# A gated mix of a long convolution and a spectral filter: channel transforms folded twice in f32, first stage and short convolution on 32x32 tiles, an order table for the planner

## The chip, the cores and the metric

The kernel runs on one core of one Trainium2 chip. Its five engines work side by side and meet through semaphores: TensorE (PE, with its weight loads shown as PEld), VectorE (DVE), ScalarE (ACT), GpSimd (POOL) and SyncE (SP), which issues the transfers. Each engine takes its instructions in the order in which they stand in the program. The metric is the device time of one execution in microseconds (us); lower is better.

## The reference

The input x = A_q has 2048 tokens of 640 channels. Path A is a gated long convolution along the tokens, path B a two-dimensional spectral filter of the same x, and a sigmoid of x mixes the two:

```python
g = _sigmoid((x * gate_w).sum(-1, keepdims=True))
a = _A_ref(x, A_k, A_v, A_shift_k, A_ssm_k, A_ssm_D)
b = _B_ref(x, B_w_r, B_w_i)
return g * a + (1 - g) * b
```

In path A, `k` goes through a causal convolution of four taps for each channel (`A_shift_k`), is multiplied by `v`, goes through a causal convolution of 2048 taps for each channel (an FFT of length 4096 in the reference, with `A_ssm_k`), gets `kv * A_ssm_D` added, and is multiplied by `q`. In path B, `rfft2` over tokens and channels is multiplied by `w_r + 1j * w_i` and taken back by `irfft2`. Everything is float32.

## The kernel before

The token transforms of length 2048 are split as 64 x 32, and every transform is a matmul with a constant matrix. A token is 32 n1 + n2; n2 is split in two halves of 16.

**Path B** runs once over all channels. `dfwd` (lines 469 to 498) takes two of 32 token columns at a time, 16 units in all. It transforms the 640 channels: a fold of the channels (d with d + 320) on POOL or DVE, line 470; then the folded tile is split into a high part (ACT, line 471) and a low part (line 472), and three matmuls in the type fp32r, high by high, low by high and high by low, stand for one in float32 (line 486). The logit of the gate comes out as one more column and is copied by DVE (line 491); ACT moves the rest to the array `XX` (line 498). Then come a first token stage (`b1`, matmul 526, transposing move by DVE 530), a second with the filter weights (`bs2`: matmul 546, two DVE products 553, two POOL sums 557), and the way back (`i1`: matmul 406, DVE transpose 411). `bfin_front` (matmuls 589 and 593) and `bfin` make the 16 output rows: again a split into high and low (ACT 598, DVE 599), 18 fp32r matmuls for each row (line 617), the scaling by 1 - g (ACT 621, DVE 623), the sum with path A on POOL (line 631), and the store.

**Path A** runs in five chunks of 128 channels. `kv` does the four taps in the layout channel by token: ACT takes the first tap (line 644), DVE the other three as scalar-tensor-tensor operations of 1024 elements (line 646), POOL multiplies by `v` (line 649; DVE in the first chunk), PE transposes (line 654), ACT moves (line 657). `s1` is the first token stage of the data and of the filter: four units each, each two matmuls on 64 x 128 tiles of the array (line 674) and one DVE transpose (line 677). `amid` is the second stage and the spectral product: 64 x 32 tiles (line 703), ACT copy 708, four DVE products 710, two POOL sums 717 with the result in the filter's array `YH`. `is1a` (406, 411) and `afin` (744, 747) go back to tokens. The two arrays `Y` and `YH` are the halves of `YY`, so a chunk's transforms wait for the readers of the chunk before.

The two paths meet through DRAM: path A writes to a scratch array `mad` that `bfin` loads again (line 628), or, where the path-A part comes late, `bfin` writes to `bfd` and `afin` loads that (line 750).

What sets the order: every operation is recorded with its engine, a cost and a due time (`DUE`, `OFF`), and `_Plan.order` runs them through a list scheduler with 8 PSUM banks and pools of SBUF buffers. What comes out is the order of the instructions on each engine.

One matmul of the program in float32 is two MATMUL instructions in the profile (line 703 is run 640 times by the program and stands there with x1280); one in fp32r is one.

## Time and profile before

| what | value |
|---|---|
| time, median of 3 runs (lowest, highest) | 361.31 us (360.91, 362.24) |
| profiled execution, first to last instruction | 362.2 us |
| PE busy | 300.0 us, 83% |
| DVE busy | 270.3 us, 75% |
| POOL busy | 203.6 us, 56% |
| ACT busy | 125.1 us, 35% |
| transfers | 66.89 MB, mean 185 GB/s |
| granted TensorE clock, mean | 0.959 of full speed |

The page has no other time of the profiled execution than its span, which lies between the lowest and the highest of the runs. Busy times are unions: instructions of one engine that overlap are counted once in an engine's total, but the groups by line count each for themselves, so their sum is a little above the total. A matmul's mean duration is from start to end and overlaps with its neighbours; what a group of matmuls costs is its busy time divided by the count.

### The profile page before, as it was taken

Reading aid. Unit: us, or ns where it says so; the run is one execution under the profiler, and the core shown is the slowest. Engines: PE = TensorE matmul, PEld = TensorE weight load, DVE = VectorE, ACT = ScalarE, POOL = GpSimd, SP = SyncE. Lnnn points to the kernel's source line nnn. Section 1 sums busy time; section 2 is a strip of 40 time slices with the busy share of each in tenths; the row PEclk is TensorE's granted clock in tenths of the full one; section 3 lists DMA queues with packets and bytes.
Section 4 is the critical chain, followed back from the end, with each engine's and each line's share of the span. In section 5 each row is a group of like instructions: output and inputs, shape, how many; then the busy total and the mean of one; then the engine's idle time right before and its main releaser. Section 6 shows DMA issues by size and latency. Waiting matters only on the chain.

```text
span 362.2 us, 9119 instructions
## 1 busy us (share of the span) xinstructions
PE 300.0 (83%) x3868; PEld 203.2 (56%) x3868; DVE 270.3 (75%) x304; ACT 125.1 (35%) x215; POOL 203.6 (56%) x173
## 2 busy tenths in 40 slices
...
GB/s 251 417 408 393 323 157 65 209 181 331 235 264 139 105 104 218 354 152 306 123 107 263 18 284 71 25 110 130 268 202 4 132 128 77 26 193 287 138 116 72
DMA packets 31591, 66.89 MB, mean 185 GB/s; under 512 B 2368, under 2 KB 15424, under 8 KB 30912
## 3 DMA queue, kind: packets, MB, share of 16 engines
q1 hardware_dynamic: 29840, 62.38, 51.4%
...
## 4 chain that ended last, share of the span: by engine, by line
PE 45%; DVE 22%; POOL 11%; DMA 9%; issue 6%; ACT 5%; SPq 0%; DVEq 0%; POOLq 0%; ACTq 0%
PE banks L617 11%; PE banks L703 6%; POOL YY L717 6%; PE banks L486 6%; PE banks L674 6%; DVE acc L646 5%; PE banks L406 4%; PE banks L589 4%; PE banks L744 3%; PE banks L526 3%; DVE YY L677 3%; DVE t L710 3%; DMA xl<-w 3%; DMA afin<-q 3%; ACT XX L498 2%
## 5 line engine op out<-in xcount | busy, mean ns | idle before, releaser
L717 POOL TENSOR_TENSOR YY<-t,t 128x512 f32<-128x512 f32 x40 | 55.9, 1416 | 28.6 <-DVE t L710 28.5
L486 PE MATMUL banks<-c,xr 128*128 128x324 f32 x288 | 51.4, 326 | 4.9 <-DVE YY L677 1.4
L710 DVE TENSOR_TENSOR t<-banks,hs 128x512 f32<-128x512 f32 x80 | 50.2, 679 | 6.1 <-ACT hs L708 5.4
L486 PEld LDWEIGHTS banks<-c,xr 128*128 128x128 f32 x288 | 43.7, 191 | 18.7 <-issue 10.0
L646 DVE SCALAR_TENSOR_TENSOR acc<-k,one,acc 128x1024 f32<-128x1024 f32 x27 | 47.4, 1755 | 8.9 <-ACT acc L644 8.7
L677 DVE STREAM_TRANSPOSE YY<-banks 128x1024 f32<-128x1024 f32 x40 | 47.7, 1226 | 7.4 <-PE banks L674 7.4
L703 PE MATMUL banks<-YY,s2a 64*32 64x256 f32 x1280 | 44.0, 406 | 9.2 <-DVE YY L677 2.3
L617 PE MATMUL banks<-c,xr 128*128 128x320 f32 x288 | 45.7, 318 | 2.6 <-DVE xr L599 2.6
L708 ACT ACTIVATE hs<-banks 128x512 f32<-128x512 f32 x40 | 23.9, 598 | 69.2 <-PE banks L703 52.5
L617 PEld LDWEIGHTS banks<-c,xr 128*128 128x128 f32 x288 | 43.6, 193 | 5.4 <-DVE xr L599 4.8
L498 ACT ACTIVATE XX<-banks 64x322 f32<-64x322 f32 x64 | 29.4, 460 | 31.3 <-PE banks L486 24.6
L472 POOL TENSOR_TENSOR xr<-xf,xr 128x384 fp32r<-128x384 f32 x30 | 33.5, 1130 | 10.5 <-ACT xr L471 10.3
L703 PEld LDWEIGHTS banks<-YY,s2a 64*32 64x32 f32 x1280 | 24.2, 109 | 25.6 <-DVE YY L677 3.7
L470 POOL TENSOR_TENSOR xf<-xl 128x384 f32<-128x384 f32 x30 | 34.9, 1170 | 6.2 <-DMA xl<-xT 6.0
L674 PE MATMUL banks<-hf,one 64*128 64x512 f32 x80 | 22.4, 668 | 19.2 <-POOL hf L684 13.9
L557 POOL TENSOR_TENSOR XX<-t,t 128x322 f32<-128x322 f32 x32 | 29.5, 940 | 13.1 <-DVE t L553 11.3
L684 POOL TENSOR_TENSOR hf<-hf 1x64 f32<-1x64 f32 x10 | 6.8, 680 | 41.5 <-PE banks L703 23.9
L406 PE MATMUL banks<-YY,one 32*64 32x512 f32 x320 | 23.9, 718 | 5.4 <-DVE YY L411 3.2
L553 DVE TENSOR_TENSOR t<-banks,xl 128x644 f32<-128x644 f32 x32 | 24.8, 811 | 3.5 <-POOL YY L717 2.0
L471 ACT ACTIVATE xr<-xf 128x384 fp32r<-128x384 f32 x32 | 16.4, 521 | 30.7 <-POOL xf L470 17.3
L411 DVE STREAM_TRANSPOSE YY<-banks 128x2048 f32<-128x2048 f32 x10 | 22.9, 2308 | 4.0 <-PE banks L406 4.0
L649 POOL TENSOR_TENSOR acc<-acc,v 128x1024 f32<-128x1024 f32 x8 | 19.0, 2379 | 11.2 <-PE banks L703 8.4
...
## 6 DMA issues: line engine op xcount, KB each, us to landing
...
k<-k SPq DMA_DIRECT2D x9, 704.0 KB, 5.1
...
q<-q SPq DMA_DIRECT2D x10, 512.0 KB, 5.4
v<-v SPq DMA_DIRECT2D x9, 512.0 KB, 5.9
afin<-q SPq DMA_DIRECT2D x9, 512.0 KB, 4.5
...
```

The source lines that it names most:

```text
L406: mm(p[h * 64:h * 64 + 64, j, :nd * 8], is1[r, ri, :], v[r, h * 2 + ri, :, d0:d0 + nd, :].rearrange("p m d e -> p d m e"), start=(ri == 0) ...
L470: lambda: o(sb(f, 3, 128), sb(x, 6, 128)[:, :3], sb(x, 6, 128)[:, 3:], op=OP.subtract if z else OP.add), r=[x], w=[f], new=[f, fh, fl])
L472: op(e, pool_us(384) if pool else 0.55, lambda: o(sb(fl, 384), sb(f, 384), sb(fh, 384), op=OP.subtract), r=[f, fh], w=[fl])
L486: mm(ps(p)[:, e, :NF], u[:, cj], dfc()[:, z, hl, cj, :], start=(i == 0), stop=(i == 8))
L498: act(XX[q, (b * 16 + n0) // 2, z * 161:z * 161 + 161, :].rearrange("p c e -> p e c"), src[:, :, ri * 161:ri * 161 + 161], AF.Copy)
L617: mm(eo[:, bank, :320], u[:, o:o + 128], dic()[:, hl, bank * 3 + cj, :], start=(i == 0), stop=(i == 8))
L646: op("DVE", dvs(1024), lambda j=j: stt(sb(acc, 8, 128), K(j), sh[:, c, j:j + 1], sb(acc, 8, 128), op0=OP.mult, op1=OP.add), r=[k, "one"], ...
L674: mm(ps(p)[:, b], m1[r], v[r], start=True, stop=True)
L677: op("DVE", dve(1024), lambda: nc.vector.transpose(by_col(dst, u * 32, 32), ps(p).rearrange("p b (d n) -> p d b n", n=16)), r=[p], w=YR(s, ...
L703: mm(ps(p)[j * 32:j * 32 + 32, h].rearrange("p (y r d) -> p y r d", y=2, r=2)[:, :, ri], s2a[r, k, ri * 32:ri * 32 + 32], YY[r, :, k // 2, ...
L710: op("DVE", dve(512), lambda x=x, t=t, p=p, hs=hs, e=e: tt(V(sb(t, 4, 256)[:, 2 * e:2 * e + 2]), V(ps(p)[:, :, :256]), V(sb(hs, 2, 256))[: ...
L717: op("POOL", pool_us(512), lambda ri=ri, o=o, dst=dst: ptt(dst(), T(t1, ri), T(t2, 1 - ri), op=o), r=[t1, t2], w=[("YH", m, u) for u in ra ...
```

## The change

The file is rewritten around the same transforms. What it does:

- **Channel transforms.** `fwd` takes four token columns at a time (8 units in place of 16). It folds the channels twice: 640 to 2 x 320 to 4 x 160, with four sums or differences of 640 elements (`ttop`, lines 282 and 284 of the new file). The matmuls are plain float32, on 64 x 128 pieces with 64 output partitions (line 290) and 32 x 64 tiles for the last 32 channels (line 297). The split into high and low is gone from here and from the output rows. `dic` makes two rows at a time: 8 matmuls of 160 columns and 8 on 32 x 128 tiles (lines 417, 423), ACT 430, four DVE operations 435, two sums 438. The logits of the gate are moved by ACT (line 304) and summed by four small matmuls.
- **Short convolution.** `kv` does the four taps on PE: 64 matmuls with diagonal 32 x 32 weights on all 16 tiles of 32 x 32 (line 461), accumulated in four banks. DVE multiplies by `v` out of PSUM (469); two sums of 512 elements fold the tokens (472); DVE transposes within SBUF (473). The ACT and DVE taps, the POOL product, the PE transposes and the ACT move are gone.
- **First stage.** The fold halves the transform. One unit is 16 matmuls of 512 columns on 32 x 32 tiles (line 500); there are two units each for data and filter in place of four. DVE moves the results by transposes of 2048 (504) or 1024 elements (508). `hf` folds the filter (485), and DVE adds `A_ssm_D` (482).
- **Arrays.** `YY` has three arrays that the chunks use in turn.
- **Stores.** Path A stores to the output for the first three chunks; path B adds to that by an accumulating transfer from the POOL queue (line 442), and stores the other two chunks, to which path A adds by accumulating transfers of 512 KB with runs of 512 bytes (line 576). The scratch arrays, their transfers and the POOL sums are gone.
- **Sums on two engines.** 144 fold and product sums go through `ttop`: 37 of them stand on DVE by a table (`ON_DVE`), the others on POOL.
- **Order.** `ORDER` and `SLOTS` are tables; there is no scheduler.
- `amid` (now `s2`), `is1a`, `afin`, `b1`, `bs2`, `i1` and `bfin_front` (now `bu`) keep their matmuls. `bs2` has 8 units of all 321 columns in place of 16 of half. ACT multiplies q by the gate, eight operations of 128 elements for each tile (line 559).

The core of the diff:

```diff
+ON_DVE = {(n, i, k) for n, l in {
+    "fwd": [(0, 1), (0, 4), (1, 3), (2, 1), (3, 1), (3, 2), (4, 2), (4, 3), (4, 4), (6, 2), (7, 2), (7, 3)],
...
+    "s2": [(0, 9), (2, 8), (2, 9), (3, 9), (5, 9), (6, 8), (8, 8), (8, 9), (10, 8), (12, 8), (14, 9), (18, 8), (18, 9)],
+    "dic": [(0, 9), (2, 8), (5, 8)],
...
+    def ttop(n, fn, **kw):
+
+        o = op("POOL", pool_us(n), None, **kw)
+        o.alt = dvs(n)
+        if o.key in ON_DVE:
+            o.eng, o.us = "DVE", dvs(n)
...
-    def dfwd_front(z, n):
...
-        op(e, pool_us(384) if pool else 0.55,
-           lambda: o(sb(f, 3, 128), sb(x, 6, 128)[:, :3], sb(x, 6, 128)[:, 3:], op=OP.subtract if z else OP.add), r=[x], w=[f], new=[f, fh, fl])
-        op("ACT", 0.52, lambda: act(sb(fh, 384), sb(f, 384), AF.Copy), r=[f], w=[fh])
-        op(e, pool_us(384) if pool else 0.55, lambda: o(sb(fl, 384), sb(f, 384), sb(fh, 384), op=OP.subtract), r=[f, fh], w=[fl])
...
-            h_, l_ = (sb(t, 3, 128) for t in fr[e])
-            i = 0
-            for cj in range(3):
-                for u, hl in ((h_, 0), (l_, 0), (h_, 1)):
-                    mm(ps(p)[:, e, :NF], u[:, cj], dfc()[:, z, hl, cj, :], start=(i == 0), stop=(i == 8))
...
+    def fwd(u):
+
+        unit("fwd", u)
+        x, y, p = new("L"), new("M"), [new("ps", 2), new("ps", 2)]
+        X = lambda b: sb(b, 4, 320)
+        op("SP", ISS, lambda: dma(sb(x, 1280), I["xT"][u]), w=[x], kb=655)
+        for o in (OP.add, OP.subtract):
+            ttop(640, lambda f, o=o: f(X(y)[:, (2 if o == OP.subtract else 0):][:, :2], X(x)[:, :2], X(x)[:, 2:], op=o), r=[x], w=[y])
+        for o in (OP.add, OP.subtract):
+            ttop(640, lambda f, o=o: f(X(x)[:, (2 if o == OP.subtract else 0):][:, :2], X(y)[:, 0::2], X(y)[:, 1::2], op=o), r=[y], w=[x])
+        blk = ((0, 0, 0, 162), (3, 1, 0, 162), (2, 0, 162, 161), (1, 1, 162, 161))
...
+        def pe():
+            for g_ in range(4):
+                for s, ri, o, n in blk:
+                    mm(bk(p, g_)[ri * 64:ri * 64 + 64, o:o + n], X(x)[:, s, g_ * 64:g_ * 64 + 64], df[:, 0, ri * 323 + o:ri * 323 + o + n],
...
+
+        def rest():
+            for s, ri, o, n in blk:
+                for g_ in range(4):
+                    r = slice(g_ * 32, g_ * 32 + 32)
...
+                       start=False, stop=(o > 0), tile_position=(g_ * 32, ri * 64))
...
+    def dic(v, ub):
+        unit("dic", v)
+        p, e_, t, bf = [new("ps", 2), new("ps", 2)], new("M"), new("M"), new("M")
...
+            for n in range(2):
+                U = sb(ub, 2, 640)[:, n, :512].rearrange("p (t r k) -> p t r k", t=2, r=2)
+                for b, (t_, r_) in enumerate(order):
+                    mm(bk(p, b)[:, n * 160:n * 160 + 160], U[:, t_, r_], di[:, b * 160:b * 160 + 160], start=(n == 0), stop=False)
+
+        def rest():
+            for n in range(2):
+                for b in range(4):
+                    r = slice(b * 32, b * 32 + 32)
+                    mm(bk(p, b)[:, n * 160:n * 160 + 160], sb(ub, 2, 640)[r, n, 512:], di[r, 640:800], start=False, stop=(n == 1),
+                       tile_position=(b * 32, 0))
...
+        nf = FIRST * 128
+        if nf:
+            op("POOL", 1.1, lambda: nc.gpsimd.dma_start(out[:, n0:n0 + 2, :nf], sb(bf, 2, 640)[:, :, :nf], accum_op=OP.add),
+               r=[bf] + [("oA", c, v // 4) for c in range(FIRST)], kb=1024)
+        if nf < D:
...
-    def kv(c, h, kvt):
...
-        op("ACT", 1.25, lambda: act(sb(acc, 8, 128), K(0), AF.Copy, scale=sh[:, c, 0:1]), r=[k, "one"], w=[acc], new=[acc])
-        for j in range(1, 4):
-            op("DVE", dvs(1024), lambda j=j: stt(sb(acc, 8, 128), K(j), sh[:, c, j:j + 1], sb(acc, 8, 128), op0=OP.mult, op1=OP.add),
-               r=[k, "one"], w=[acc])
...
+    def kv(c):
+        unit("kv", c)
+        k, p = new("G"), [new("ps", 2), new("ps", 2)]
+        vs = [new("V") for _ in range(2)]
+        op("SP", ISS, lambda: dma(sb(k, 2240), I["k"][c]), w=[k], kb=1147)
+        for a in range(2):
+            op("SP", ISS, lambda a=a: dma(sb(vs[a], 1024), I["v"][c, a]), w=[vs[a]], kb=524)
...
+            for tp in range(4):
+                for i in range(4):
+                    r = slice(i * 32, i * 32 + 32)
+                    for j in range(4):
+                        o = (8 * j + 3 - tp) * 64
+                        mm(bk(p, i)[j * 32:j * 32 + 32, :], dg[r, c, tp], sb(k, 2240)[r, o:o + 512], start=(tp == 0), stop=(tp == 3),
+                           tile_position=(i * 32, j * 32))
+
+        op("PE", 4 * mmu(512), pe, r=[k, "ca"], w=p, mode="32x32")
+        sds = []
+        for a in range(2):
+            v_, f_, sd = vs[a], new("T"), new("T")
+            sds.append(sd)
+            op("DVE", dve(1024), lambda a=a, v_=v_: tt(sb(v_, 2, 512), ps(p[a]), sb(v_, 2, 512), op=OP.mult), r=[p[a]], w=[v_])
+            V = lambda v_=v_: sb(v_, 16, 2, 32)
+            for s, o in enumerate((OP.add, OP.subtract)):
+                ttop(512, lambda f, s=s, o=o, V=V, f_=f_: f(sb(f_, 2, 16, 32)[:, s], V()[:, :, 0], V()[:, :, 1], op=o), r=[v_], w=[f_])
+            op("DVE", dve(1024), lambda f_=f_, sd=sd: nc.vector.transpose(sb(sd, 4, 32, 8).rearrange("p i c n -> p i n c"),
+                                                                         sb(f_, 4, 8, 32)), r=[f_], w=[sd])
+        return sds
...
+    def hf(c, a):
...
+        for s, o in enumerate((OP.add, OP.subtract)):
+            ttop(512, lambda f, s=s, o=o: f(sb(sd, 2, 512)[:, s], sb(raw, 2, 512)[:, 0], sb(raw, 2, 512)[:, 1], op=o), r=[raw], w=[sd])
+        return sd
...
-    def s1(c, s, buf, dst, u):
...
-                r = slice(b * 64, b * 64 + 64)
-                mm(ps(p)[:, b], m1[r], v[r], start=True, stop=True)
...
+    def s1(nm, c, a, sd, y):
...
+            for s in range(2):
+                for j in range(4):
+                    r = slice(j * 32, j * 32 + 32)
+                    o = ps(p[0])[:, j] if nm == "s1Y" else bk(p, j)
+                    for h in range(2):
+                        q = (h * 2 + s) * 32
+                        mm(o[q:q + 32, :], m1[r, q:q + 32], sb(sd, 2, 512)[r, s], start=True, stop=True, tile_position=(j * 32, q))
...
+        op("PE", mmu(512), pe, r=[sd, "ca"], w=p, mode="32x32")
...
+        cs = slice(c * 128, c * 128 + 128)
+        if c < FIRST:
+            op("SP", ISS, lambda: dma(out[:, n0:n0 + 8, cs], Q()), r=[qt], w=[("oA", c, n0 // 8)], kb=524)
...
+            op("POOL", 1.1, lambda: nc.gpsimd.dma_start(out[:, n0:n0 + 8, cs], Q(), accum_op=OP.add),
+               r=[qt] + [("oB", v) for v in range(n0 // 2, n0 // 2 + 4)], kb=800)
...
+    slots = iter(SLOTS)
+    for b in plan.bufs:
+        b.slot = next(slots)
     with tc.manual_schedule():
-        for o in ops:
-            o.fn()
+        for i in ORDER:
+            plan.ops[i].fn()
```

What the tables make of the order is seen at three places. On DVE at the start, before, the names are the taps of the first chunk (`acc`, `q`), the input tile `k` and the gate columns `gs`:

```order
L646 SCALAR_TENSOR_TENSOR acc_63<-k_61,one,acc_63 128x1024
L423 TENSOR_SCALAR gs<-one 128x3
L424 SCALAR_TENSOR_TENSOR gs<-one,gs 128x2
L425 SCALAR_TENSOR_TENSOR gs<-one,gs 128x2
L426 TENSOR_SCALAR gs<-one,two 128x1
L427 TENSOR_TENSOR gs<-gs 128x1
L646 SCALAR_TENSOR_TENSOR q_84<-c_86,one,q_84 128x1024
L646 SCALAR_TENSOR_TENSOR acc_63<-k_61,one,acc_63 128x1024
```

In the changed kernel `V` holds v and the product, `L` and `M` the folds of x, `cc` and `gt` the gate columns, `T` the folded tokens:

```order
L469 TENSOR_TENSOR V_69<-banks,V_69 128x1024
L282 TENSOR_TENSOR M_64<-L_62 128x640
L267 TENSOR_SCALAR cc<-cc 128x8
L268 TENSOR_TENSOR gt<-cc 128x2x2
L269 TENSOR_TENSOR gt<-cc 128x2x2
L270 TENSOR_TENSOR cc<-gt 128x2x2
L271 TENSOR_TENSOR cc<-gt 128x2x2
L284 TENSOR_TENSOR L_62<-M_64 128x640
L469 TENSOR_TENSOR V_70<-banks,V_70 128x1024
L284 TENSOR_TENSOR L_62<-M_64 128x640
L473 STREAM_TRANSPOSE T_74<-T_72 128x4x8x32
```

The first DVE instruction was a tap that needs a loaded tile and ACT's first tap; now it is the product out of PSUM, which needs PE's 64 matmuls of the short convolution.

On DVE in the second stage of the first chunk, before; `t` are the products, `xf` and `xr` the folded channels and their low part, `lg` the logits:

```order
L710 TENSOR_TENSOR t_80<-banks,hs_77 128x512
L710 TENSOR_TENSOR t_79<-banks,hs_78 128x512
L710 TENSOR_TENSOR t_80<-banks,hs_78 128x512
L710 TENSOR_TENSOR t_81<-banks,hs_77 128x512
L470 TENSOR_TENSOR xf_71<-xl_76 128x384
L710 TENSOR_TENSOR t_82<-banks,hs_77 128x512
L710 TENSOR_TENSOR t_81<-banks,hs_78 128x512
L472 TENSOR_TENSOR xr_70<-xf_71,xr_69 128x384
L491 COPY lg<-banks 128x2
L710 TENSOR_TENSOR t_82<-banks,hs_78 128x512
```

And now, where line 541 is the sum of products that stood on POOL, 282 a channel fold, 482 and 485 work on the filter:

```order
L534 TENSOR_TENSOR M_66<-banks,H_77 128x512
L534 TENSOR_TENSOR M_67<-banks,H_77 128x512
L482 TENSOR_TENSOR V_70<-V_70 128x16
L282 TENSOR_TENSOR M_65<-L_63 128x640
L534 TENSOR_TENSOR M_67<-banks,H_76 128x512
L485 TENSOR_TENSOR T_73<-V_70 128x512
L534 TENSOR_TENSOR M_68<-banks,H_77 128x512
L482 TENSOR_TENSOR V_71<-V_71 128x16
L534 TENSOR_TENSOR M_64<-banks,H_77 128x512
L534 TENSOR_TENSOR M_66<-banks,H_76 128x512
L541 TENSOR_TENSOR YY<-M_66,M_67 128x2x2x128
```

The copies of the logits are gone from between the products; sums and folds that read two SBUF tiles have come there.

On POOL at the end, before, `v` and `acc` hold path B's rows and `xl` path A's:

```order
L631 TENSOR_TENSOR acc_63<-acc_63,xl_76 128x512
L631 TENSOR_TENSOR v_62<-v_62,xl_75 128x512
L751 TENSOR_TENSOR q_83<-q_83,hf_65 128x1024
L631 TENSOR_TENSOR v_62<-v_62,xl_73 128x640
L631 TENSOR_TENSOR acc_63<-acc_63,xl_75 128x640
L631 TENSOR_TENSOR v_62<-v_62,xl_73 128x640
L631 TENSOR_TENSOR acc_63<-acc_63,xl_76 128x640
L631 TENSOR_TENSOR v_62<-v_62,xl_74 128x640
```

And now, where 442 and 576 are the accumulating transfers, 438 the sums of path B's rows and 541 the sums of products of the last chunk:

```order
L442 DMA out_dram<-M_66 128x2x384
L541 TENSOR_TENSOR YY<-M_64,M_68 128x2x2x128
L438 TENSOR_TENSOR M_64<-M_67 128x2x320 x2
L442 DMA out_dram<-M_64 128x2x384
L541 TENSOR_TENSOR YY<-M_68,M_66 128x2x2x128 x2
L541 TENSOR_TENSOR YY<-M_65,M_67 128x2x2x128 x2
L576 DMA out_dram<-V_70 128x8x128
L576 DMA out_dram<-V_69 128x8x128
L541 TENSOR_TENSOR YY<-M_66,M_68 128x2x2x128 x2
L576 DMA out_dram<-V_71 128x8x128
L576 DMA out_dram<-V_70 128x8x128
```

The last four accumulating transfers stand in POOL's queue around the last sums of products; before, POOL's end held path-B sums alone, and the stores went out from SP.

882 lines of the change are left out of this document (305 added, 577 removed), and 39 rows, old and new, of tables (ORDER, SLOTS).

## The prediction

> **What bounds the kernel now.** I read the busy time by stage first, then the waits, then the groups by line. The table by stage has a row for each stretch, and in it the busy us of each engine with its instructions; the last row has the totals.
>
> ```profile
> core 0: us, PE busy (x) PEld busy (x) DVE busy (x) ACT busy (x) POOL busy (x), PEclk, DMA share, GB/s
> 0.00:8.00 8.00, 0.00 (x0) 0.00 (x0) 0.00 (x0) 2.40 (x3) 0.20 (x4) 1.00 0.75 252
> 8.00:270.00 262.00, 215.94 (x2828) 130.02 (x2836) 220.94 (x234) 90.18 (x162) 171.30 (x146) 0.95 0.62 207
> 270.00:358.00 88.00, 84.08 (x1050) 73.20 (x1032) 48.57 (x71) 32.54 (x52) 32.14 (x23) 0.98 0.36 117
> 358.00:362.30 4.30, 0.00 (x0) 0.00 (x0) 0.80 (x1) 0.00 (x0) 0.00 (x0) 0.70 0.20 76
> sum 362.30, PE 300.02 PEld 203.22 DVE 270.32 ACT 125.12 POOL 203.65; mean PE 75.01 PEld 50.81 DVE 67.58 ACT 31.28 POOL 50.91
> ```
>
> Nothing runs on PE and DVE in the first 8 us. From 8 to 270 us PE (215.9 of 262) and DVE (220.9) are almost equally full, with POOL at 171.3, a share of 0.65. From 270 to 358 us PE alone is the bound: 84.1 of 88, a share of 0.955, and DVE is half idle. So in three quarters of the span a gain on one engine alone is worth little, and in the last quarter only PE counts. The longest wait of DVE in the table of waits is this:
>
> ```profile
> DVE lg L491 <- ACT XX L498: 13.7, 8, 2.2
> ```
>
> DVE's copy of the gate's logit stands in its queue behind ACT's move of the same banks, and DVE is idle 13.7 us for it. Without that wait DVE's share from 8 to 270 us is 220.9 / (262 - 13.7) = 0.89.
>
> One more thing bounds DVE. In the timeline from 100 to 112 us, start and duration in the first two columns, a tap on DVE that reads two SBUF tiles lasts 5.78 us while POOL runs one operation after the other:
>
> ```profile
> 103.81 5.78 DVE L646 SCALAR_TENSOR_TENSOR acc<-k,one,acc 128x1024 f32<-128x1024 f32 x1
> ...
> 105.30 1.27 POOL L717 TENSOR_TENSOR YY<-t,t 128x512 f32<-128x512 f32 x1
> ...
> 106.53 1.97 POOL L470 TENSOR_TENSOR xf<-xl 128x384 f32<-128x384 f32 x2
> ...
> 108.47 1.32 POOL L684 TENSOR_TENSOR hf<-hf 1x64 f32<-1x64 f32 x1
> ```
>
> DVE's products that read PSUM do not stretch: the view of line 710 has their shortest, median and longest within 46 ns.
>
> ```profile
> L710 DVE TENSOR_TENSOR t<-banks,hs x80: 647/680/693, 34.6 to 299.2; 128x512 f32<-128x512 f32 x80
> ```
>
> **The change part by part.** PE, from the groups by line (busy us, then mean ns of one):
>
> ```profile
> L486 PE MATMUL banks<-c,xr 128*128 128x324 f32 x288 | 51.4, 326 | 4.9 <-DVE YY L677 1.4 <-issue 1.2 <-DVE YY L411 0.9
> ...
> L617 PE MATMUL banks<-c,xr 128*128 128x320 f32 x288 | 45.7, 318 | 2.6 <-DVE xr L599 2.6
> L703 PE MATMUL banks<-YY,s2a 64*32 64x256 f32 x1280 | 44.0, 406 | 9.2 <-DVE YY L677 2.3 <-ACT XX L498 2.0 <-DVE lg L491 1.9
> ...
> L406 PE MATMUL banks<-YY,one 32*64 32x512 f32 x320 | 23.9, 718 | 5.4 <-DVE YY L411 3.2 <-DVE lg L491 2.2
> ...
> L674 PE MATMUL banks<-hf,one 64*128 64x512 f32 x80 | 22.4, 668 | 19.2 <-POOL hf L684 13.9 <-DVE lg L491 3.0 <-DVE YY L677 2.3
> L674 PE MATMUL banks<-kvt,one 64*128 64x512 f32 x80 | 21.5, 662 | 1.9 <-ACT XX L498 1.3 <-DVE YY L677 0.3 <-ACT kvt L657 0.2
> L744 PE MATMUL banks<-YY,is2a 128*64 128x128 f32 x320 | 19.7, 277 | 0.9 <-DVE YY L411 0.9
> ...
> L589 PE MATMUL banks<-c,XX 128*128 128x128 f32 x128 | 18.8, 290 | 0.0
> ...
> L654 PE MATMUL banks<-one,acc 128*128 128x128 f32 x72 | 10.0, 284 | 3.8 <-POOL acc L649 2.3 <-DVE t L553 1.1 <-DVE YY L677 0.4
> ```
>
> The fp32r transforms (51.4 and 45.7), the first stage (22.4 and 21.5) and the transposes (10.0) go: 151.0 of 300.0, leaving 149.0. What comes is float32, two passes for each matmul.
> - Folded forward transform, 8 units: 16 matmuls of 162 columns that run in pairs. Line 744 runs pairs of 128 columns at 19.7 / 160 = 0.123 us a pass, so 162 cost 0.156, and 8 pairs in 2 passes 2.49 us. The rest is 2 sets of 8 tiles of 32 x 64; line 406 runs such a set of 512 columns in 23.9 / 40 = 0.597 us, so 162 cost 0.189, four times 0.76. Together 3.25 x 8 = 26.0.
> - Output rows, 8 units: 16 passes of 160 columns at line 589's 18.8 / 128 = 0.147 us for 128, so 2.94; the rest on four row tiles 4 x 0.187 = 0.75. 3.69 x 8 = 29.5.
> - Short convolution and first stage: packs of 16 tiles of 32 x 32, which no row shows. The nearest have 8 tiles: 0.597 a pass in line 406, and 44.0 / 160 = 0.275 for 256 columns in line 703, so 0.55 for 512. I take 0.575, as the tiles have run side by side in both. Below it stands 21.5 / 40 = 0.54, a stream of 512 columns in line 674; above it 1.19, if 8 tiles run and then the other 8. The convolution has 8 passes (4.6 us), five times: 23.0. The first stage has 20 units of 2 passes: 23.0.
>
> PE's sum is 149.0 + 101.5 = 250.5 us; with the bounds 248 to 300.
>
> The Trainium skill, in "TensorE: Matmul & The Clock Gate", section "Measured speedup vs the span model", gives 16 tiles of 32 x 32 a speedup of 10.6, not 16, so a pack lasts 1.51 single matmuls. With line 589's rate (0.588 for 512 columns) that is an estimate of 0.89 a pass and a PE sum of 275.5; no run here shows it yet.
>
> DVE and what bears on it:
>
> ```profile
> L677 DVE STREAM_TRANSPOSE YY<-banks 128x1024 f32<-128x1024 f32 x40 | 47.7, 1226 | 7.4 <-PE banks L674 7.4
> L646 DVE SCALAR_TENSOR_TENSOR acc<-k,one,acc 128x1024 f32<-128x1024 f32 x27 | 47.4, 1755 | 8.9 <-ACT acc L644 8.7
> ...
> L599 DVE TENSOR_TENSOR xr<-banks,xr 128x640 fp32r<-128x640 f32 x16 | 13.1, 822 | 10.6 <-ACT xr L598 10.5
> ...
> L747 DVE TENSOR_TENSOR q<-banks,q 128x1024 f32<-128x1024 f32 x10 | 12.2, 1215 | 1.9 <-PE banks L744 1.9
> ...
> L646 DVE SCALAR_TENSOR_TENSOR q<-c,one,q 128x1024 f32<-128x1024 f32 x3 | 3.8, 1278 | 0.0
> ...
> L491 DVE COPY lg<-banks 128x2 f32<-128x2 f32 x16 | 2.4, 149 | 14.9 <-ACT XX L498 13.7 <-PE banks L674 0.9 <-PE banks L486 0.3
> L445 DVE TENSOR_TENSOR c<-gs,c 128x2 fp32r<-128x2 f32 x4 | 2.4, 631 | 0.0
> L470 DVE TENSOR_TENSOR xf<-xl 128x384 f32<-128x384 f32 x2 | 2.0, 1016 | 0.0
> L649 DVE TENSOR_TENSOR q<-q,q 128x1024 f32<-128x1024 f32 x1 | 2.0, 2014 | 0.0
> ...
> L631 DVE TENSOR_TENSOR acc<-acc,xl 128x640 f32<-128x640 f32 x1 | 0.8, 826 | 0.0
> ```
>
> The taps (47.4, 3.8), the low parts (13.1), the logits (2.4) and the early small groups (2.4, 2.0, 2.0) go: 73.1 of 270.3, leaving 197.2. Still smaller groups that also go are left in, so this errs high. Added are ten products out of PSUM (1.215 each, line 747: 12.2), ten transposes in SBUF (none in the trace; 47.7 / 40 = 1.19 by line 677: 11.9), and 37 sums that read two SBUF tiles: 16 of 640 at 0.825 (line 631 on DVE, POOL idle then), 21 of 512 in proportion at 0.66, and ten tiny ones at 0.15, together 28.6. That is 249.9 us before the loss to POOL. A tap into `acc` has a mean of 1755 ns, and the three into `q`, in the first chunk when POOL has hardly begun, 1278: some 0.48 us each are lost while POOL works. The transposes, products and `bs2` that stay keep their price.
>
> POOL, which these 47 operations meet:
>
> ```profile
> L717 POOL TENSOR_TENSOR YY<-t,t 128x512 f32<-128x512 f32 x40 | 55.9, 1416 | 28.6 <-DVE t L710 28.5 <-PE banks L674 0.2
> ...
> L631 POOL TENSOR_TENSOR v<-v,xl 128x640 f32<-128x640 f32 x3 | 4.7, 1563 | 11.2 <-DVE v L623 10.3 <-ACT xl L629 1.0
> ...
> L453 POOL DMA_DIRECT2D c<-dfc x2 | 1.9, 938 | 0.0
> ```
>
> It has 27 sums at 1.416, 33 of 640 at 1.56, 15 of 642 at the same, 32 of 512 at 1.25 and 12 transfers to issue at 0.94: 38 + 52 + 23 + 40 + 11 = 164 us, a share of 0.51 in some 323 us. The loss of 0.48 us was at 0.65; at 0.51 it is 0.375, and 47 times that is 17.6. DVE's sum is 267.5; with the bounds of no loss and of one whole POOL operation (1.56) each, 250 to 323.
>
> The Trainium skill, in "SBUF — State Buffer", section "SBUF: two separate sides", says that DVE and GpSimd share a pair of ports under an exclusive lock, which a DVE operation takes if it has two SBUF inputs. The 5.78 us row agrees; by the rule the ten transposes in SBUF are spared, and if they were not, they would add an estimated 10 x 0.375 = 3.8 us.
>
> The start and the end:
>
> ```profile
> 1.65 0.42 SPq L641 DMA_DIRECT2D c<-k  x1
> ...
> 13.88 3.79 PE L674 MATMUL banks<-hf,one 64*128 64x512 f32 x8 [13.88 <-POOL hf L684]
> ```
>
> ```profile
> c<-dfc POOLq DMA_DIRECT2D x2, 966.0 KB, 18.3
> ...
> c<-k SPq DMA_DIRECT2D x1, 704.0 KB, 6.2
> ...
> out_dram<-q SPq DMA_DIRECT2D x1, 512.0 KB, 3.8
> ```
>
> ```profile
> 358.83 0.33 SPq L632 DMA_DIRECT2D out_dram<-acc  x1
> ```
>
> The third transfer of 704 KB, behind some 0.9 MB, lands at 1.65 + 6.2 = 7.85 us, 1.6 MB in all. The constants and k of the changed kernel are 448 and 1120 KB by their tiles, so PE can begin at 7.7. Its 4.6 us become 6.2, as the first eight matmuls of line 674 took 3.79 us in place of 8 x 0.27. DVE's first instruction waits for that: 13.9 us, in place of some 8. POOL's folds and the loads run meanwhile, but nothing on DVE does.
>
> At the end the last store was issued at 358.83, and the span is 362.2: 3.4 us. Now POOL issues it (0.94) and it adds to what is there. Such a landing is not in the trace: a plain store of the same 512 KB took 3.8, a POOL transfer in the crowded start 18.3. I take two plain landings, 7.6, as it moves the old values too; the end is 8.5 us (4.7 to 19).
>
> At no cost I count the accumulating transfers that wait in POOL's queue for path A's stores: what stands behind them are folds of the next chunk, and POOL is half idle; uncovered, the first costs a landing, 3.8 us. The scratch transfers that go were hidden, with the DMA engines at 0.62. ACT (125 us) loses more than it gets.
>
> **The sum.** The engines are now evenly loaded to the end, so the stage from 270 us goes, and the stage before is the pattern. With the logit's wait gone, the next to be late for DVE are ACT's copies of the products, which remain. DVE: 267.5 / 0.89 + 13.9 + 8.5 = 323 us. PE, as a check: 250.5 / (215.9 / 262 = 0.824) + 7.7 + 8.5 + 1.2 for the last product = 321. I forecast 323. The page gives no time of the profiled execution but its span, 362.2, which is 0.9 above the median of 361.31; that is below what I can resolve.
>
> **The rivals.**
> - *Better packed.* The table order fills DVE as the last stage filled PE, 0.955: 267.5 / 0.955 + 22.4 = 303 us. For it speaks that POOL has slack now; against it that PE and DVE are both nearly full, and that convolution, transforms and first stage take four of eight banks where most took two.
> - *Tiles by halves, the case on the other side.* The 16 tiles run 8 at a time, on PE in lines 461 and 500. 80 passes x 0.615 = 49 us: PE 299.5 / 0.824 + 17.4 = 381 us, slower. It decides from a PE sum of (362.2 - 17.4) x 0.824 = 284, which is 0.99 us a pass. For it: nothing here runs more than 8. Against it: 8 tiles cost no more than one stream. By the skill's 0.89 the time would be an estimated 352, between the two.
> - *DVE starves behind POOL.* Every one of the 47 waits out a whole POOL operation: 323 / 0.89 + 22.4 = 385 us. It decides from 1.1 us each. Against it: a loss of 0.48 at a busier POOL.
> - *No gain*: the old share of 0.843 stays and several ends add up, about 361.
>
> **How the numbers follow.** The forecast has 0.64 (from 303, no loss to POOL, to 340, DVE's share at 220.9 / 262 = 0.843), better packed 0.20, tiles 0.08, starving 0.06, no gain 0.02. The range of 298 to 350 holds the forecast and most of the better case; the three others and the far tail of the better one stay outside. A measurement can tell about 0.5%, 1.8 us, from no change. Faster takes the first two and the milder end of the tiles: 0.86; same 0.03; slower 0.11.
>
> **What would show it.** Right: DVE busy about 268 and PE about 250 us; the convolution at 4.6 us for 128 matmuls and the first stage at 1.15 for 32; the DVE sums of 512 at about 1.0 us; DVE's first operation near 14 us; 8 to 9 us from the last product to the end. Wrong: packs above 1 us a pass; DVE sums that stretch over whole runs of POOL; a share of DVE below 0.8 or above 0.95 after the start.

## The result and the profile after

The changed kernel takes 348.52 us (median of three runs, 345.36 to 350.55) against 361.31 before. The ratio is 0.962, with a 95% interval of 0.953 to 0.972; one of the three runs was disturbed and is not in it. The forecast was 323: the direction was right, and the gain is 13 us in place of 38. The profiled execution is the one of 345.36 us, with a span of 343.6.

The page of the changed kernel begins with the span and the busy time of each engine:

```profile
span 343.6 us, 10756 instructions
...
PE 266.1 (77%) x4850; PEld 155.4 (45%) x4850; DVE 263.0 (77%) x282; ACT 81.4 (24%) x188; POOL 170.5 (50%) x123
```

The sums of work are near those of the forecast: PE 266.1 (250.5 forecast, bounds 248 to 300), DVE 263.0 (267.5), POOL 170.5 (164). The table by stage is cut where DVE's first and last operations stand:

```profile
core 0: us, PE busy (x) PEld busy (x) DVE busy (x) ACT busy (x) POOL busy (x), PEclk, DMA share, GB/s
0.00:12.90 12.90, 5.84 (x128) 2.52 (x128) 0.00 (x0) 0.00 (x0) 1.76 (x5) 1.00 0.87 340
12.90:270.00 257.10, 211.68 (x3746) 124.58 (x3754) 211.51 (x220) 61.25 (x141) 129.04 (x89) 0.94 0.48 155
270.00:334.30 64.30, 48.58 (x992) 28.28 (x974) 51.45 (x64) 20.20 (x47) 38.16 (x28) 0.97 0.39 75
334.30:343.60 9.30, 0.00 (x0) 0.00 (x0) 0.02 (x1) 0.00 (x0) 1.56 (x2) 0.69 0.96 113
```

DVE begins at 12.9 us (13.9 forecast) and the end is 9.3 us (8.5 forecast). Between them DVE works 211.5 + 51.5 of 321.4 us, a share of 0.818 where the forecast had 0.89. PE's share from its first matmul at 7.1 to its last at 333.0 is 266.1 / 325.9 = 0.816. Two engines are equally full, and each is idle nearly a fifth of the time. If their intervals are laid over one another, neither runs for 18.8 us, nearly all of it at the start and the end, so both run together for 266.1 + 263.0 - (343.6 - 18.8) = 204.3 us, PE alone for 62 and DVE alone for 59. Between start and end there is hardly a moment in which both are idle, but for 121 us only one of them works: they take turns.

DVE's waits in the changed kernel (us in total, times, longest):

```profile
DVE V L469 <- PE banks L461: 17.7, 5, 12.9
DVE M L534 <- ACT H L532: 9.7, 12, 2.4
DVE XX L339 <- PE banks L335: 9.5, 7, 6.3
DVE YY L508 <- PE banks L500: 8.8, 5, 3.0
DVE V L571 <- PE banks L568: 7.3, 5, 2.3
```

The wait for ACT at the logit, 13.7 us before, is gone. In its place stand many waits for PE, at nearly every step that reads PSUM. The groups that the forecast priced without a row (busy us, mean ns, idle before):

```profile
L500 PE MATMUL banks<-T,ca 32*32 32x512 f32 x640 | 30.9, 641 | 11.0 <-DVE XX L259 3.2 <-ACT lg L304 2.0 <-DVE M L534 1.9
...
L461 PE MATMUL banks<-G,ca 32*32 32x512 f32 x640 | 25.1, 633 | 8.7 <-DMA G<-k 7.1 <-DVE M L361 1.0 <-DVE YY L508 0.7
...
L473 DVE STREAM_TRANSPOSE T<-T 128x1024 f32<-128x1024 f32 x10 | 20.4, 2072 | 0.1
...
L541 DVE TENSOR_TENSOR YY<-M,M 128x512 f32<-128x512 f32 x13 | 11.9, 924 | 0.1
...
L442 POOL DMA_DIRECT2D out_dram<-M x8 | 10.2, 1277 | 1.5 <-POOL M L438 1.5
...
L576 POOL DMA_DIRECT2D out_dram<-V x4 | 6.2, 1597 | 12.9 <-DVE V L571 12.9
```

The first stage costs 30.9 / 20 = 1.55 us a unit in place of 1.15, and the convolution 5.0 in place of 4.6. For the first stage the timeline of the changed kernel tells why; the first two columns are the start and the duration:

```profile
59.96 0.15 PEld L500 LDWEIGHTS banks<-T,ca 32*32 32x32 f32 x8 [0.23 <-issue]
59.96 2.14 PE L500 MATMUL banks<-T,ca 32*32 32x512 f32 x32
...
60.98 0.21 PEld L500 LDWEIGHTS banks<-T,ca 32*32 32x32 f32 x24 [0.87 <-ACT XX L305]
...
295.49 1.16 PE L500 MATMUL banks<-T,ca 32*32 32x512 f32 x32
```

At 295.5 us the pack of 16 tiles runs as one and takes 1.16 us, the forecast's price. At 60.0 only a part of it starts, and the rest waits until ACT has emptied its bank. The stream is then paid twice, 2.14. Banks are not the only reason: at 75.0 us the second half waits for a sum of POOL. Twelve of the twenty units take 1.14 to 1.25 us, two some 1.9 (at a granted clock of 0.57 from 184 to 188 us), and six, which start in parts or while a convolution still runs, 1.8 to 3.1 of busy time. The five convolutions take 5.84, 4.64, 5.42, 4.46 and 4.79 us; matmuls of the first one last up to 1058 ns, those of the other four 587 to 612.

The clock has a part in PE's sum. By its records in the trace PE worked some 29 of its 266 us at half clock (26 of 300 before), and there a matmul of line 500 lasts 945 to 1056 ns in place of 584 to 612.

The last chunk of the changed kernel is a chain with nothing beside it:

```profile
319.41 1.86 DVE L541 TENSOR_TENSOR YY<-M,M 128x512 f32<-128x512 f32 x2
...
320.82 5.39 PE L254 MATMUL banks<-YY,ca 32*64 32x512 f32 x64 [4.57 <-DVE YY L541]
...
324.58 4.51 DVE L259 STREAM_TRANSPOSE YY<-banks 128x2048 f32<-128x2048 f32 x2 [3.30 <-PE banks L254]
...
329.15 3.85 PE L568 MATMUL banks<-YY,is2a 128*64 128x128 f32 x64 [2.94 <-DVE YY L259]
331.23 1.23 DVE L571 TENSOR_TENSOR V<-banks,V 128x1024 f32<-128x1024 f32 x1 [2.14 <-PE banks L568]
...
334.62 1.55 POOL L576 DMA_DIRECT2D out_dram<-V  x1 [0.31 <-DVE V L571]
```

### The profile page after: what moved, and what is told of

Its sections match the earlier page's. It is cut to its first block, busy times and chain, and to the rows that moved or that the text cites. A ratio compares the mean times of both kernels' runs of the same rounds, so it can differ in the third digit from the quotient of the medians.

```text
span 343.6 us, 10756 instructions
## 1 busy us (share of the span) xinstructions
PE 266.1 (77%) x4850; PEld 155.4 (45%) x4850; DVE 263.0 (77%) x282; ACT 81.4 (24%) x188; POOL 170.5 (50%) x123
## 5 line engine op out<-in xcount | busy, mean ns | idle before, releaser
L534 DVE TENSOR_TENSOR M<-banks,H 128x512 f32<-128x512 f32 x80 | 50.6, 683 | 10.0 <-ACT H L532 9.7
L541 POOL TENSOR_TENSOR YY<-M,M 128x512 f32<-128x512 f32 x27 | 38.9, 1460 | 23.3 <-DVE M L534 20.8
L527 PE MATMUL banks<-YY,s2a 64*32 64x256 f32 x1280 | 44.3, 402 | 5.2 <-DVE YY L508 2.5
L532 ACT ACTIVATE H<-banks 128x512 f32<-128x512 f32 x40 | 23.9, 598 | 71.5 <-PE banks L527 55.3
L438 POOL TENSOR_TENSOR M<-M 128x640 f32<-128x640 f32 x13 | 20.7, 1590 | 38.8 <-DVE M L435 27.3
L559 ACT ACTIVATE V<-V,g 128x128 f32<-128x128 f32 x80 | 24.2, 388 | 66.1 <-DMA V<-q 66.1
L500 PE MATMUL banks<-T,ca 32*32 32x512 f32 x640 | 30.9, 641 | 11.0 <-DVE XX L259 3.2
L485 POOL TENSOR_TENSOR T<-V 128x512 f32<-128x512 f32 x18 | 25.0, 1398 | 24.2 <-DVE V L482 22.4
L254 PE MATMUL banks<-YY,ca 32*64 32x512 f32 x320 | 25.8, 690 | 9.3 <-DVE YY L541 4.6
L461 PE MATMUL banks<-G,ca 32*32 32x512 f32 x640 | 25.1, 633 | 8.7 <-DMA G<-k 7.1
L508 DVE STREAM_TRANSPOSE YY<-banks 128x1024 f32<-128x1024 f32 x20 | 24.3, 1231 | 8.8 <-PE banks L500 8.8
L472 POOL TENSOR_TENSOR T<-V 128x512 f32<-128x512 f32 x14 | 21.5, 1543 | 13.4 <-DVE V L469 13.4
L361 DVE TENSOR_TENSOR M<-banks,L 128x642 f32<-128x642 f32 x32 | 24.1, 813 | 1.0 <-DMA L<-w 0.5
L504 DVE STREAM_TRANSPOSE YY<-banks 128x2048 f32<-128x2048 f32 x10 | 23.0, 2305 | 1.6 <-PE banks L500 1.5
```

What stands on the lines that cost most here:

```text
L254: mm(p[h * 64:h * 64 + 64, j, :nd * 8], is1[r, ri, :], v[r, h * 2 + ri, :, d0:d0 + nd, :].rearrange("p m d e -> p d m e"), start=(ri == 0) ...
L461: mm(bk(p, i)[j * 32:j * 32 + 32, :], dg[r, c, tp], sb(k, 2240)[r, o:o + 512], start=(tp == 0), stop=(tp == 3), tile_position=(i * 32, j * ...
L485: ttop(512, lambda f, s=s, o=o: f(sb(sd, 2, 512)[:, s], sb(raw, 2, 512)[:, 0], sb(raw, 2, 512)[:, 1], op=o), r=[raw], w=[sd])
L500: mm(o[q:q + 32, :], m1[r, q:q + 32], sb(sd, 2, 512)[r, s], start=True, stop=True, tile_position=(j * 32, q))
L504: op("DVE", dve(2048), lambda: nc.vector.transpose(by_col(YY[:, :, y], a * 64, 64), ps(p[0]).rearrange("p j (d n) -> p d j n", n=8)), r=p, ...
L508: op("DVE", dve(1024), lambda b=b: nc.vector.transpose(by_col(YY[:, :, y], a * 64 + b * 32, 32), ps(p[b]).rearrange("p q (d n) -> p (q d) ...
```

## The experiments

All ratios are to the kernel before, on the same chip; the changed kernel stands at 0.962 (0.953 to 0.972). The differences show only the parts that change, with long lines shortened.

**What bounds it: less work on one engine.** The first run takes work from PE.

```diff
-            for tp in range(4):
+            for tp in range(2):
...
-            for s, ri, o, n in blk:
+            for s, ri, o, n in ():
...
-            for n in range(2):
+            for n in ():
```

> The changed kernel with less work on PE and the same instructions elsewhere: the convolution has two taps of four, and the second part of the forward transform (line 297) and of the output rows (line 423) is left out. By the groups of the changed kernel that is 25.1 / 2 = 12.5, 8.2 and 6.4 us, 27 of PE's 266. The changed kernel takes 345 to 349 us. DVE bounds it, as forecast, and PE has slack: no more than 2 us less, 343 to 348. PE bounds it: 27 / 0.83 = 32 less, about 314. They run in turn, as the eight banks let neither run far ahead (in the trace PE runs alone 62 us, DVE alone 59, both together 204): each us counts between 0.23 (62 / 266) and a half, 6 to 14 less, 332 to 341.

Measured: 338.22 us, 0.933 (0.927 to 0.938).

```profile
PE 248.6 (74%) x4146; PEld 140.5 (42%) x4146; DVE 261.6 (78%) x282; ACT 82.0 (24%) x188; POOL 169.9 (51%) x123
```

PE's busy time fell by 17.5 us (not by the 27 that the groups had promised), and the span by 8.1, to 335.5: 0.46 for each. The second run takes work from DVE (the memsets at the start only give the tiles a value, 3.6 us in time in which DVE would wait).

```diff
-nc.vector.transpose(sb(sd, 4, 32, 8).rearrange("p i c n -> p i n c"), sb(f_, 4, 8, 32))
+nc.vector.transpose(sb(sd, 1024)[:, :32], sb(f_, 1024)[:, :32])
...
+        for t in plan.T:
+            tc.nc.vector.memset(t, 0.0)
```

> The changed kernel with less work on DVE and the same instructions elsewhere: the ten transposes in SBUF (line 473, 2.07 us each) move 32 elements of 1024, so the first stage of path A reads old data. That is some 19 of DVE's 263 us. DVE bounds it: 19 / 0.82 = 23 less, 322 to 326. PE bounds it: nothing, 344 to 349. In turn: each us counts between 0.22 (59 / 263) and a half, 4 to 10 less, 336 to 344.

Measured: 343.18 us, 0.949 (0.945 to 0.954), a span of 340.2.

```profile
PE 263.2 (77%) x4850; PEld 154.7 (45%) x4850; DVE 249.9 (73%) x286; ACT 81.4 (24%) x188; POOL 171.1 (50%) x123
```

Without the memsets DVE lost 16.7 us and the span 3.4: 0.2 for each. By the medians the two figures are 0.59 and 0.32; the runs of the changed kernel lie 5 us apart, so they are rough, and which engine's us weighs more is not firm. Neither engine bounds the kernel alone; both "in turn" numbers came. The forecast's formula, DVE's sum over a fixed share, would have given 20 us here.

**The sums' engine.**

```diff
-ON_DVE = {(n, i, k) for n, l in {
...
-}.items() for i, k in l}
+ON_DVE = set()
```

> The changed kernel with all 144 folding sums on POOL, in the same order: DVE loses 37 sums, 37.9 of 263 us, and POOL gets 37 times some 1.45, 54 more, 224 in all. DVE bounds it: 37.9 / 0.82 = 46 less, about 300. In turn, with POOL in nobody's way: 8 to 19 less, 328 to 340. The sums' own length counts, as each sum that was put on DVE is one that the next stage waits for (0.9 there, 1.45 on POOL, and behind what POOL has in its queue): 0 to 15 more, 346 to 362.

Measured: 357.45 us, 0.986 (0.981 to 0.990), 9 slower than the changed kernel.

```profile
PE 272.4 (77%) x4850; PEld 158.8 (45%) x4850; DVE 236.4 (66%) x245; ACT 81.7 (23%) x188; POOL 210.9 (59%) x160
```

DVE has 26.6 us less to do and the kernel is slower. Its table of waits says where the time goes (line 277 is 284 of the changed kernel):

```profile
PEld banks L283 <- POOL L L277: 14.4, 7, 7.8
...
PE banks L283 <- POOL L L277: 10.7, 5, 6.9
...
DVE T L466 <- POOL T L465: 8.2, 5, 2.3
```

In the changed kernel PE's matmuls wait 3 us for POOL in all, and DVE not at all. Here, what counts is when a sum is ready for the step behind it, not whose busy time it is in.

**The accumulating transfers.**

```diff
-op("POOL", 1.1, lambda: nc.gpsimd.dma_start(out[:, n0:n0 + 8, cs], Q(), accum_op=OP.add),
+op("SP", ISS, lambda: dma(out[:, n0:n0 + 8, cs], Q()),
...
-op("POOL", 1.1, lambda: nc.gpsimd.dma_start(out[:, n0:n0 + 2, :nf], sb(bf, 2, 640)[:, :, :nf], accum_op=OP.add),
+op("SP", ISS, lambda: dma(out[:, n0:n0 + 2, :nf], sb(bf, 2, 640)[:, :, :nf]),
```

> The changed kernel with the twelve accumulating transfers of POOL made plain stores that SP issues, so the output holds one path's part only and not the sum. POOL loses 16.4 us of issues, and the last store lands as a plain one. The end alone counts: 1.56 to issue and 6.9 to land become 0.4 and 4.1, 4 less, 341 to 345. The queue counts too (DVE waits 4.5 us for an M buffer that such a transfer reads, and folds stand behind the transfers on POOL): 8 to 14 less, 331 to 339. Nothing less: the last landing is not what ends the span, 344 to 349.

Measured: 342.07 us, 0.944 (0.940 to 0.949). The span after DVE's last operation is 4.1 us in place of 9.3, so 5.2 of the 6 us between the medians are the end itself, as the first theory had it. The two profiled spans are only 2.2 apart (341.4 and 343.6): what lies ahead of the end is 3 us longer here. So nothing shows that the transfers' wait in POOL's queue costs time, as forecast.

**The step that gave 0.89, tried alone in the kernel before.**

```diff
-op("DVE", 0.16, lambda: nc.vector.tensor_copy(lg[:, z, n0:n0 + 2], ps(p)[:, :, 322]),
+op("DVE", 0.16, lambda: act(lg[:, z, n0:n0 + 2], ps(p)[:, :, 322], AF.Copy),
```

> The kernel before, with the copy of the gate's logit (line 491) on ACT in place of DVE; the order of everything else stays. This tries the step of the forecast that took DVE's wait of 13.7 us as time that is free once the copy leaves DVE. If it is free, DVE's share from 8 to 270 us becomes 0.89 and the kernel before takes 361.3 - 13.7 = 348. If the wait is only where DVE stands while PE and ACT are behind, it moves to the next instruction of DVE, and the time is 357 to 362.

The "DVE" in the call is a label of the planner; in the profile the sixteen copies run on ACT.

Measured: 361.14 us, 0.997 (0.994 to 1.000). Its longest waits of DVE, and its stage from 8 to 270 us:

```profile
DVE v L623 <- PE banks L617: 11.9, 6, 3.5
DVE YY L677 <- PE banks L674: 10.9, 7, 5.2
DVE xr L599 <- ACT xr L598: 10.5, 13, 1.0
...
DVE t L710 <- ACT hs L708: 7.1, 9, 2.4
```

```profile
8.00:270.00 262.00, 219.84 (x2908) 131.54 (x2908) 223.88 (x220) 92.36 (x179) 170.83 (x146) 0.96 0.61 207
```

The wait of 13.7 us is gone from the table, and the time stays. DVE's share in this stage went from 0.843 to 223.9 / 262 = 0.855, not to 0.89. The idle time moved to the next instructions that need PE: the transposes of line 677 wait 10.9 us where they waited 7.4.

**The order.** The whole table is worked out anew, by moving single steps, buffers and sums between places and keeping what made a timetable of the measured lengths shorter. The steps are the same. Not all stand on the same engine, though: 29 of the folding sums are on DVE in place of 37, and only nine of these are the same ones. Steps 226 to 232 are the filter's load, its folds and its first stage.

```diff
-ORDER = [
-    2, 203, 205, 51, 0, 204, 226, 206, 7, 6, 52, 211, 212, 53, 287,
...
+ORDER = [226, 227, 228, 229, 51, 2, 230, 231, 232, 52, 53, 54, 55, 203,
...
-SLOTS = [
-    1, 1, 0, 6, 0, 1, 0, 6, 0, 2, 4, 6, 0, 3, 0, 2, 0, 0, 0, 2, 1, 3,
...
+SLOTS = [0, 3, 4, 6, 1, 0, 6, 2, 1, 3, 0, 2, 1, 2, 4, 2, 1, 4, 4, 6, 0, 0,
```

> The changed kernel with the same instructions in another order, with other buffers and with 29 of the folding sums on DVE in place of 37: the table was worked out anew by the lengths that the trace of the changed kernel shows. The lengths written in the code make PE's sum 205 us where the trace shows 266 (the convolution 3.4 in place of 5.0, the first stage 0.85 in place of 1.5, a transpose in SBUF 1.22 in place of 2.07). If the table's wrong lengths are why PE and DVE run in turn, the time falls by 20 to 29, to 320 to 329, with PE and DVE together for over 215 us in place of 204. If the eight banks and the chain of the steps make them run in turn whatever the order, 340 to 349.

Measured: 323.04 us, 0.891 (0.887 to 0.895). This kernel's lines are 48 lower, as its tables are shorter (437 is 485 of the changed kernel). Its page, its stage between DVE's first and last operations, and its start:

```profile
PE 259.0 (80%) x4850; PEld 151.8 (47%) x4850; DVE 257.6 (80%) x274; ACT 81.3 (25%) x188; POOL 180.1 (56%) x131
```

```profile
4.70:313.80 309.10, 259.04 (x4850) 151.81 (x4850) 257.46 (x274) 80.04 (x187) 178.32 (x126) 0.96 0.52 156
```

```profile
4.77 1.29 DVE L437 TENSOR_TENSOR T<-V 128x512 f32<-128x512 f32 x2
...
7.34 2.02 PE L452 MATMUL banks<-T,ca 32*32 32x512 f32 x32 [7.34 <-DMA ca<-ca]
...
9.46 2.38 DVE L460 STREAM_TRANSPOSE YY<-banks 128x1024 f32<-128x1024 f32 x2 [3.41 <-PE banks L452]
...
11.90 5.82 PE L413 MATMUL banks<-G,ca 32*32 32x512 f32 x128 [2.53 <-DVE YY L460]
...
17.76 1.23 DVE L421 TENSOR_TENSOR V<-banks,V 128x1024 f32<-128x1024 f32 x1 [1.60 <-PE banks L413]
```

The first transfer is now a filter of 520 KB; in the changed kernel the constants (448 KB) and k (1120 KB) come first. DVE folds the filter at 4.8 us, the first stage runs at 7.3 when the constants have landed, and the convolution follows at 11.9, behind DVE's move of the first stage's result. Both engines together: 259.0 + 257.6 - (321.9 - 17.3) = 212 us. The overlap grew by 8 and not by the 11 that I named, but the sums on PE and DVE shrank by 7 and 5 us too. On DVE there are fewer sums. On PE it is not the packs (lines 461 and 500 had 56.1 us, and have 57.7 here) but lines 254 and 527, which fell from 38.8 and 44.3 us to 33.1 and 41.6. The granted clock does not explain the gain: 0.947 here, 0.942 in the changed kernel. What the sums' new engines are worth without the new order was not tried; all of them on POOL was slower, as above.

**The control: the same search with the lengths of the code.**

```diff
-    2, 203, 205, 51, 0, 204, 226, 206, 7, 6, 52, 211, 212, 53, 287,
...
+    51, 52, 226, 7, 227, 228, 229, 2, 230, 203, 53, 206, 54, 8, 9, 10,
```

> The control to the run with the table worked out anew: the same search, as long and from the same start, but with the lengths that stand in the code (205 us for PE) in place of those of the trace; the instructions are the same, 31 of the folding sums stand on DVE. If the wrong lengths made the table of the changed kernel slow, this one is slow too, 340 to 349. If the table was only searched too little, or for queues and transfers that behave otherwise than the chip's, most of the gain comes here as well, 323 to 332, and the right lengths are worth only what is left.

Measured: 326.80 us, 0.902 (0.895 to 0.909).

```profile
4.70:312.50 307.80, 254.93 (x4850) 146.08 (x4850) 265.94 (x276) 81.18 (x188) 177.92 (x124) 0.98 0.52 156
```

My reason for the new table was wrong: the lengths in the code are not what held the table back. With them the search finds nearly all of the gain (the intervals of the two ratios just touch, 0.887 to 0.895 and 0.895 to 0.909). This table has 31 sums on DVE, and its profiled execution had more clock, 0.970. The table of the changed kernel, with its choice of engines for the sums, is simply a poor one for its work.

**Start and rest.** The first 70 steps of the changed kernel's table are kept, and the rest is worked out anew.

```diff
-    291, 17, 223, 32, 224, 301, 33, 292, 225, 293, 302, 247,
...
+    291, 17, 223, 32, 33, 292, 34, 224, 225, 63, 64, 35,
```

> The changed kernel's instructions with the first 70 steps of its table kept as they are (so DVE still waits for the first convolution, some 13 us) and the rest of the table worked out anew by the lengths of the trace, as in the run that took 323.0. In that run DVE's first operation came at 4.8 us in place of 12.9, and from DVE's first operation to its last it was 309 us in place of 321. If both parts add up, this run keeps the 12 and gives back the 8: 330 to 333. If the start alone made the difference, 340 to 348. If DVE's late start is made up for later, 322 to 327.

Measured: 333.08 us; the ratio is 0.927 with a wide interval (0.899 to 0.955), as runs on this chip scattered more.

```profile
14.90:323.00 308.10, 259.23 (x4722) 152.89 (x4722) 267.41 (x279) 79.53 (x187) 170.14 (x120) 0.93 0.48 142
```

By the median both parts add up, as 330 to 333 was the expectation for that; the interval alone would allow the other two theories as well. In the profiled executions from DVE's first operation to its last it is 308.1 us in place of 321.4, and the late start remains (14.9). This table has 34 sums on DVE. Here DVE's share is 267.4 / 308.1 = 0.868.

**The transposes in SBUF.** The sources of the changed kernel by shortest, median and longest (ns):

```profile
L473 DVE STREAM_TRANSPOSE T<-T x10: 1976/2064/2215, 20.1 to 267.4; 128x1024 f32<-128x1024 f32 x10
```

```profile
L541 DVE TENSOR_TENSOR YY<-M,M x13: 645/694/1772, 60.9 to 320.6; 128x512 f32<-128x512 f32 x13
```

The sums of two SBUF tiles stretch to 2.7 times their shortest; the transposes hardly at all. They cost 2.06 us always, so this is not POOL. One run writes half of them densely.

```diff
-sb(sd, 4, 32, 8).rearrange("p i c n -> p i n c")
+sb(sd, 4, 32, 8).rearrange("p i c n -> p i n c") if a else sb(sd, 4, 8, 32)
```

> The changed kernel with half of the transposes in SBUF (line 473, the first of each chunk's two) writing their 1024 columns one after another in place of every eighth column, so the first stage of path A reads its columns in another order. If the stride makes them cost 2.06 us in place of 1.22 (line 508, out of PSUM), the five dense ones take about 1.2 and the five others 2.06. If it is the source in SBUF, all ten stay at 2.0 to 2.1. The time falls by 0 to 2, 343 to 349.

Measured, one run: 349.15 us. In its timeline a strided one and a dense one stand three us apart:

```profile
20.34 2.05 DVE L473 STREAM_TRANSPOSE T<-T 128x1024 f32<-128x1024 f32 x1
...
23.02 1.25 DVE L473 STREAM_TRANSPOSE T<-T 128x1024 f32<-128x1024 f32 x1
```

The five dense ones take 1.20 to 1.25 and the others 2.04 to 2.14. It is the stride of the write (eight elements, 32 bytes), neither the source nor the lock. The next run uses that, and lets PE read with the stride.

```diff
-sb(sd, 2, 512)[r, s]
+sb(sd, 4, 8, 32)[r, 2 * s:2 * s + 2].rearrange("p i n c -> p i c n")
```

> The changed kernel, its order kept, with all ten transposes in SBUF (line 473) writing one column after another, and the first stage of path A (line 500) reading every 32nd column in its place, so that the result stays the reference's. DVE loses 10 x 0.85 = 8.5 us. In turn, at 0.22 to 0.5 for each us: 2 to 4 less, 341 to 346. DVE bounds it: 10 less, 335 to 339. If PE reads with a stride at a lower rate, the ten units of line 500 grow (1.15 undisturbed) and the gain is lost, 346 to 352.

Measured: 351.40 us, 0.974 (0.967 to 0.980): nothing gained.

```profile
L500 PE MATMUL banks<-T,ca 32*32 32x512 f32 x640 | 39.5, 836 | 10.4 <-DVE XX L259 2.9 <-DVE M L534 2.1 <-ACT lg L304 2.0
...
L473 DVE STREAM_TRANSPOSE T<-T 128x1024 f32<-128x1024 f32 x10 | 12.1, 1220 | 0.8 <-POOL T L472 0.8
```

DVE saves 8.3 us and PE pays 8.6: undisturbed units of path A take 2.1 us in place of 1.15. That fits two engines in turn, where a us on PE weighs about as much as one on DVE.

**Both together, and a variant.** The edit of the run before, and a table that starts with the filter again:

```diff
-    2, 203, 205, 51, 0, 204, 226, 206, 7, 6, 52, 211, 212, 53, 287,
...
+    226, 227, 228, 51, 52, 53, 54, 229, 2, 230, 231, 232, 203, 206,
```

> Both together: the dense transposes with the strided first stage, and a table worked out by the lengths of the trace with 1.24 for these transposes. The run with the new table alone took 323.0. If DVE's 8.5 us count as they did by turns (0.28 a us), 320 to 321; if the better packed order lets DVE bound, 8.5 / 0.87 less, 313 to 315; if the stride costs PE what it gives DVE, 322 to 326.

Measured: 314.36 us, 0.869 (0.864 to 0.874), the fastest of all and within the second range.

```profile
PE 263.6 (84%) x4850; PEld 149.6 (48%) x4850; DVE 253.1 (81%) x276; ACT 81.0 (26%) x188; POOL 176.7 (56%) x129
```

It is not shown that DVE bounds here, as that range supposed: besides the edit the table is another one, and the granted clock was 0.974 in place of 0.947 in the run of 323.0. What each is worth was not taken apart.

The variant gives the strided read to the transpose out of PSUM.

```diff
-nc.vector.transpose(by_col(YY[:, :, y], a * 64, 64), ps(p[0]).rearrange("p j (d n) -> p d j n", n=8))
+[nc.vector.transpose(by_col(YY[:, :, y], a * 64 + i * 32, 32),
+    ps(p[0])[:, :, i * 256:i * 256 + 256].rearrange("p j (n c) -> p c j n", c=32)) for i in range(2)]
```

> The ten transposes in SBUF write one column after another, as in the run of 314.4 us, but it is now the transpose out of PSUM after the first stage of path A (line 504) that reads every 32nd column, in two halves, in place of PE (a pack then cost 2.1 in place of 1.15); the table is worked out by the trace's lengths. PE gets back some 8 us of the 36 in line 500, DVE pays 0.15 for each of ten splits. If DVE reads PSUM with a stride at its usual rate: 308 to 313. If such a read costs double, as the strided write in SBUF did, DVE grows by 20 and the time is 318 to 326.

Measured: 319.74 us, 0.892 (0.880 to 0.905). That lies in the second range, but not for its reason:

```profile
L500 PE MATMUL banks<-T,ca 32*32 32x512 f32 x640 | 27.0, 622 | 15.1 <-DMA ca<-ca 10.2 <-DVE XX L259 1.9 <-DVE YY L259 1.2
...
L504 DVE STREAM_TRANSPOSE YY<-banks 128x1024 f32<-128x1024 f32 x20 | 23.6, 1223 | 1.7 <-PE banks L500 1.7
```

The read out of PSUM with the stride costs nothing (1223 ns for 1024, where 2048 without it took 2305), and PE got its time back (36.3 to 27.0 in line 500). Yet the profiled span, 313.9, is no shorter than the 313.1 of the run before, and the median is longer. PE begins 2.8 us later, and another table differs in much else; why it is not faster stays open.

## Why the prediction was wrong

The sum was DVE / share + start + end. Term by term, forecast and measured:

| term | forecast | measured |
|---|---|---|
| DVE's sum | 267.5 | 263.0 |
| of it ten transposes in SBUF | 11.9 | 20.4 (line 473) |
| of it folding sums with the loss to POOL, tiny ones included | 46.2 | 40.3 |
| of it what was kept, and the ten products | 209.4 | 202.3 |
| PE's sum | 250.5 | 266.1 |
| of it forward, rows, convolution, first stage | 26.0, 29.5, 23.0, 23.0 | 29.2, 27.2, 25.1, 30.9 |
| DVE's first operation | 13.9 | 12.9 |
| the end | 8.5 | 9.3 |
| **DVE's share between** | **0.89** | **0.818** |

With 263.0 / 0.89 + 12.9 + 9.3 the time would be 317.7; with 0.818 it is 343.6. The errors of the other terms bring the sum from 323 to 317.7, so by the formula the whole miss of 26 us between 317.7 and the profiled span is in the share. With the 0.855 that the kernel before had without the wait, the sum is 329.8: some 12 of the 26 are the step on the logit, and some 14 lie between 0.855 and 0.818, in the step that carried a share of the old order to the new one.

- **The step that failed** is "Without that wait DVE's share from 8 to 270 us is 220.9 / (262 - 13.7) = 0.89". It takes a wait out of the time as though nothing else were going on in it. In that stage of the kernel before, PE was at 215.9 of 262, and without the wait DVE waited longer for PE at the next steps instead (10.9 us in place of 7.4 at line 677). Taken alone in the kernel before, the step was worth 0.4 us by the medians and not 13.7; by the ratio's interval between nothing and 2.3.
- **The evenly loaded stage as "the pattern" to the end** failed with it. Two engines that wait for one another do not add up to one that is full; whether the eight banks set how much they overlap was not tried. A us less on PE was worth roughly 0.46, a us less on DVE roughly 0.2. I had written "a gain on one engine alone is worth little", and then divided DVE's sum alone by a share.
- **The order, which the forecast left out.** It spoke of the table in one rival only. The same work in another order, with other sums on DVE, takes 323 us: so the forecast's time can be had, but by another sum, 4.7 + 257.5 / 0.833 + 8.1, and that the two agree is luck. Of the 26 us median to median, some 10 are the start (323.0 against 333.1 with the first 70 steps kept) and some 15 the rest; the run with the start kept scattered, so this split is rough. What in the old table's rest cost the time stays open.
- **Packs of 16 tiles.** The price was right (1.14 to 1.25 in twelve units, forecast 1.15) where the pack found its four banks and its input ready; I had not thought of a pack that starts in parts. Together with the convolution, whose first unit I had priced at 6.2 us in the start (5.84 came) but at 4.6 in the sum, that is 10 of the 15.6 us that PE's sum was low. With the speedup of 10.6 that the Trainium skill gives in "TensorE: Matmul & The Clock Gate", section "Measured speedup vs the span model", the estimate was 0.89 us a pass; the 1.16 us row (two passes) gives 0.58, so the measurement decides against that estimate here. By the formula of the same section, one matmul and some 4 ns for each further tile, a pass would be an estimated 0.588 + 0.06 = 0.65 us, nearer, and still above the row.
- **DVE behind POOL.** Forecast 0.375 us a sum; the 37 sums took 37.9 us, 0.29 each above the 27.1 that they have without loss (16 x 0.825 + 21 x 0.66). The Trainium skill, in "SBUF — State Buffer", section "Who interferes with whom", exempts DVE instructions with at most one SBUF input that are not in a mode with two ports, and the transposes agree (1976 to 2215 ns, POOL busy or not). Their price was wrong for another reason: the rows that I took it from write in pairs, and none had every eighth element.
- **Rivals.** Better packed did not come with this table; a better table came to 0.864 and 0.868 of DVE. Tiles by halves did not happen as such. DVE did not starve. "No gain" had the right idea on the share, at a chance of 0.02, and the wrong time, as I added ends to it that did not come.
- **The signs that I named.** DVE's busy time, its sums of 512 (0.92 to 1.14 us), its first operation and the end came as forecast; the first stage (1.55 a unit) and PE's sum were high. The share was to be wrong below 0.8 or above 0.95, and 0.818 lies between: the one term on which the time hung had the widest test.

What three arrays in turn are worth by themselves was not tried.
